# Three transfers of one batch issued by ScalarE instead of SyncE

## The chip, the cores and the metric

The kernel runs on 1 core of a Trainium2 chip. The core has TensorE (PE in the rows; its weight loads are PEld), VectorE (DVE), ScalarE (ACT), GpSimd (POOL) and SyncE (SP), which issues transfers. The metric is device time in microseconds (us) for one execution, as a median over runs. "PEclk" or the granted clock is the share of TensorE's full clock that the chip granted in a stretch: 1.00 is the 2.4 GHz level, 0.50 the 1.2 GHz level.

## The reference

The input has 8 batches of 3136 rows of 256 numbers. Each batch goes through a Fourier transform along its rows, a complex linear layer with a soft threshold, and the inverse transform. All 25088 rows then go through one expert layer:

```python
X = np.fft.rfft(x, axis=1)
Yr = Xr @ w_r - Xi @ w_i + b_r
Yi = Xr @ w_i + Xi @ w_r + b_i
Yr = np.sign(Yr) * np.maximum(np.abs(Yr) - lam, 0.0)   # Yi likewise
y = np.fft.irfft(Y, n=x.shape[1], axis=1)
...
h = x @ w_in                                           # 256 -> 1024
solu = h * softmax(h)
ln = (solu - mean) / sqrt(var + 1e-6) * g_ln
out = ln @ w_out                                       # 1024 -> 256
```

## The kernel before

A transform of length 3136 is done as 98 times 32. For every batch `b` there are four steps: `fwd1` (matmuls of 98 rows, stored to a scratch tensor in DRAM, `s1`, called `s1f` for the first two batches), `fwd2` with `mix` (the short transform and the linear layer, tile names `pb`, `Xh16`, `y`), `inv1` (the way back's short transform, whose result goes to a second scratch tensor `s2`, called `s2f` for batch 0), and `inv2` (the way back's matmuls of 98 rows, into the buffers `ring_hi`, `ring_lo`). The expert layer then takes 128 rows at a time: `moe_head` (tile `ph`, softmax in `u`), `moe_turn` (a split in two fp16 halves and a transposing transfer into `th`, `tl`) and `moe_tail` (tile `po`, output `o`). The expert layer of batch `b` runs beside the transforms of later batches. Only batch 0 has nothing to run beside: its way back must end before the first expert matmul can begin.

The scratch `s2f` of batch 0 is written by `inv1`: 128-row pieces from tile `zout`, and last the remaining 64 rows from tile `zs` (64x256 fp32, 64 KB, L821). `inv2` reads it back in groups of four columns into tile `zt` (98x1024 fp32, 392 KB, L843); there are two `zt` buffers, so the first two groups are loaded at once and the others when a buffer is free. Each group feeds 16 of PE's matmuls `pf<-iaf_s,zt`. Beside that, in the same stretch, batch 1's `fwd1` runs (loads `xt`, 392 KB; matmuls `pf<-xt,fa_s`; copies `av` on ScalarE; stores `s1f<-av`, 392 KB), and the second expert weight is prepared in quarters of 512 KB (loads `u<-in_moe_w_out`; VectorE turns its 64-bit numbers into fp32 in `th` and `tl`, GpSimd multiplies in the sign and exponent, ScalarE multiplies by `g_ln`, "th<-th,gt" and "tl<-tl,gt").

A class `Plan` records every operation and sets the order: it keeps a model of each engine and puts an operation where its model says it would start, by due times (`nc.key`). The order is then fixed for each engine, and each engine runs its own list strictly in that order; an instruction that waits for a semaphore holds back all that stands behind it on its engine. All operations are issued by `Plan.issue`, so all rows bear its line, L342. In the kernel before every transfer is issued by SyncE, on one queue.

Of the kernel before, what the change touches and what calls it, by code (L numbers as in the profile page):

```python
# [24 lines left out]
S, N1, N2 = 3136, 98, 32  # L25
H = N1 // 2
Q = (H - 1) // 2
# [424 lines left out]
def fft_mix_solu_kernel(ctx: ExitStack, tc, x, w_r, w_i, b_r, b_i, w_in, w_out, g_ln, fa, fbf, fsf, iaf, fa16, fb, fs, gb, gs, ia, out):  # L452
    nc = Plan(tc.nc)
    B, _, D = x.shape
# [18 lines left out]
    def front_psum(b):  # L473

        return banks.tile("pf" if b else "pb")
# [165 lines left out]
    s2 = {}  # L641
# [22 lines left out]
    def unit_size(u):  # L664

        return (1, 2 * N2) if u == NU - 1 else (2, P)
# [113 lines left out]
    def inv1(b, u0, u1):  # L780


        n, _ = unit_size(u0)
        half = 2 * N2
        K = half * n
        g, gi = divmod(2 * u0, QG)
        part, dtype = ((2, D), F16) if b >= PLAIN_Z else ((D,), F32)
        if n == 1:
            zo, gi = fp.tile([K, 1, *part], dtype, name="zs", bufs=1), 0
        else:  # L790
            if gi == 0:
                zouts[b] = fp.tile([P, QG, *part], dtype, name="zout")
            zo = zouts[b]
        w = u1 - u0
        pz = [front_psum(b) for _ in range(n)]
        nc.reserve(zo[:, gi : gi + n * w])
        with nc.together():
            for u in range(u0, u1):
                yh, yl = Ys.pop((b, u))
                for k, (t, j) in enumerate(((yh, 0), (yl, 0), (yh, 1))):  # L800
                    for ri in range(2):
                        for i in range(n):
                            rows = slice(i * half, (i + 1) * half)
                            gw = gs_s[:, ri, j] if n == 1 else gb_s[g][rows, u % 2, ri, j]
                            nc.tensor.matmul(
                                pz[i][:K, (u - u0) * D : (u - u0 + 1) * D], gw, t[rows, ri], start=k + ri == 0, stop=k + ri == 3
                            )
        m = n * w
        for i in range(n):
            pv = pz[i][:K, : w * D].rearrange("p (u e) -> p u e", u=w)  # L810
            if b < PLAIN_Z:
                zv = zo[:, gi : gi + m].rearrange("p (u i) e -> p u i e", i=n)[:, :, i]
                nc.scalar.activation(zv, pv, AF.Copy, scale=Z_SCALE)
                continue
            zv = zo[:, gi : gi + m].rearrange("p (u i) t e -> p u i t e", i=n)[:, :, i]
            nc.scalar.activation(zv[:, :, 0], pv, AF.Copy, scale=Z_SCALE)
            nc.vector.scalar_tensor_tensor(zv[:, :, 1], zv[:, :, 0], -LOW, pv, ALU.mult, ALU.add)
        if b >= PLAIN_Z:
            zo = zo.rearrange("p q t e -> p q (t e)")
        if n == 1:  # L820
            nc.sync.dma_start(s2[b][4 * Q :].rearrange("c (n m) -> (c n) m", n=N2), zo[:, 0])  # L821
        else:
            v = s2[b][: 4 * Q].rearrange("(q c) m -> q (c m)", c=4).rearrange("q (r m) -> r q m", r=P)
            nc.sync.dma_start(v[:, g * QG + gi : g * QG + gi + m], zo[:, gi : gi + m])
# [5 lines left out]
    G2 = 4  # L830
# [6 lines left out]
    def inv2(b, g):  # L837
        if b >= PLAIN_Z:
            zt = fp.tile([P, G2, 2, D], F16, name="zt", bufs=2)[:N1]
            nc.sync.dma_start(zt.rearrange("c n t d -> c (n t d)"), s2[b][:, g * G2 * 2 * D : (g + 1) * G2 * 2 * D])  # L840
        else:
            zt = fp.tile([P, G2, D], F32, name="zt", bufs=2)[:N1]
            nc.sync.dma_start(zt.rearrange("c n d -> c (n d)"), s2[b][:, g * G2 * D : (g + 1) * G2 * D])  # L843
        j0 = (b * N2 + g * G2) * N96 % R
        if g == 0 and b % 2 == 0:
            lasts[b // 2] = [fp.tile([P, ND, 2, N1 - N96, N2], F16, name=f"last_{part}", bufs=1) for part in ("hi", "lo")]
        for eh in range(ND):
            pa = banks.tile("pf")
            to = [
                (  # L850
                    ring[:, eh, j0 : j0 + G2 * N96].rearrange("p (i n) -> p i n", n=N96),
                    last[:, eh, b % 2, :, g * G2 : (g + 1) * G2].rearrange("p n i -> p i n"),
                )
                for ring, last in zip((ring_hi, ring_lo), lasts[b // 2])
            ]
            nc.reserve(*to[0], *to[1])
            with nc.together():
                for i in range(G2):
                    es = slice(eh * P, (eh + 1) * P)
                    if b < PLAIN_Z:  # L860
                        nc.tensor.matmul(pa[:, i * N1 : (i + 1) * N1], zt[:, i, es], iaf_s, start=True, stop=True)
                        continue
                    for k, (t, j) in enumerate(((0, 0), (0, 1), (1, 2))):
                        nc.tensor.matmul(pa[:, i * N1 : (i + 1) * N1], zt[:, i, t, es], ia_s[:, j], start=k == 0, stop=k == 2)
            pv = pa[:, : G2 * N1].rearrange("p (i n) -> p i n", n=N1)
            for hi, lo, ns in zip(*to, (slice(0, N96), slice(N96, N1))):
                nc.scalar.activation(hi, pv[:, :, ns], AF.Copy, scale=X_SCALE)
                nc.vector.scalar_tensor_tensor(lo, hi, -LOW, pv[:, :, ns], ALU.mult, ALU.add)
# [275 lines left out]
    def front_b(b, key, step):  # L1144

        lag = 4 if b == 0 else 3
        for n in range(NU + lag):
            nc.key = key + n * step
            for fn, u in ((fwd2, n), (mix, n - 1)):
                if 0 <= u < NU:  # L1150
                    fn(b, u)
            u = n - lag
            if u == NU - 1 or 0 <= u < NU and b == 0:

                inv1(b, u, u + 1)
            elif 0 < u < NU and u % 2:
                inv1(b, u - 1, u + 1)
# [20 lines left out]
    for b in range(B):  # L1178
        L = 24 + b % 2
        if b == 0:  # L1180
            front_a(1, -40, 0.5)
        if b + 2 < B:
            front_a(b + 2, first + 6, (L - 6) / 17)
        if b + 1 < B:
            front_b(b + 1, first + (6 if b == 0 else -2), (L - (8 if b == 0 else 4)) / (NU + 3))
        groups = 0
        for n in range(L):
            while groups < N2 // G2 and groups * G2 * N96 <= n * P:
                nc.key = first + n - 3
                inv2(b, groups)  # L1190
                groups += 1
            nc.key = first + n
            heads.append(moe_head((b, n if n < 24 else None)))
            nc.key = first + n + 0.5
            turned.append(moe_turn(*heads.pop(0)))
            nc.key = first + n + 1
            moe_tail(*turned.pop(0))
        first += L
# [25 lines left out]
```

## Time and profile before

| | us |
|---|---|
| median of 3 runs | 1615.39 (1613.5 to 1616.07) |
| the profiled execution's own time | 1616.65 |
| its span, first to last instruction | 1614.9 |
| PE busy in the span | 1577.4 (98%) |
| DVE busy | 1326.1 (82%) |
| ACT busy | 1238.8 (77%) |
| POOL busy | 1123.6 (70%) |
| mean DMA rate over the span | 180 GB/s |

The shares are averages over the whole span. PE is nearly always busy from 115 us on; its largest pauses lie in the first 115 us, where weights and the first batch are on their way. What a change there is worth is read from the stretch itself: which wait ends last in it.

### The profile page before, as it was taken

Reading aid. Unit: us, or ns where it says so; the run is one execution under the profiler, and the core shown is the slowest. Engines: PE = TensorE matmul, PEld = TensorE weight load, DVE = VectorE, ACT = ScalarE, POOL = GpSimd, SP = SyncE. Lnnn points to the kernel's source line nnn. Section 1 sums busy time; section 2 is a strip of 40 time slices with the busy share of each in tenths; the row PEclk is TensorE's granted clock in tenths of the full one; section 3 lists DMA queues with packets and bytes.
Section 4 is the critical chain, followed back from the end, with each engine's and each line's share of the span. In section 5 each row is a group of like instructions: output and inputs, shape, how many; then the busy total and the mean of one; then the engine's idle time right before and its main releaser. Section 6 shows DMA issues by size and latency. Waiting matters only on the chain.

```text
span 1614.9 us, 38042 instructions
## 1 busy us (share of the span) xinstructions
PE 1577.4 (98%) x13040; PEld 1126.1 (70%) x13040; DVE 1326.1 (82%) x3423; ACT 1238.8 (77%) x2576; POOL 1123.6 (70%) x1889
## 2 busy tenths in 40 slices
PE   5979999999999999999999999999999999999998
PEld 3545877678766777667776687666876677776675
DVE  4779789996799877898789978899688888877775
ACT  4667678886789867898679876798678877778886
POOL 0555776677866777667777687766976677777676
PEclk8989999999999999999999999999999999999999
DMA  8868955996579965899669984699857986677676
GB/s 236 277 228 206 210 145 133 227 240 155 127 185 232 226 151 121 185 243 217 135 130 224 279 169 118 135 246 258 166 112 165 204 172 129 122 146 154 140 129 115
DMA packets 533923, 290.25 MB, mean 180 GB/s; under 512 B 427642, under 2 KB 503964, under 8 KB 533728
## 3 DMA queue, kind: packets, MB, share of 16 engines
q1 hardware_dynamic: 533728, 287.82, 78.5%
q8 instruction: 102, 1.67, 0.4%
q14 instruction: 93, 0.76, 0.2%
HBM read 107.89 MB, written 77.07 MB: 115 GB/s over the span
## 4 chain that ended last, share of the span: by engine, by line
PE 92%; DVE 3%; ACT 2%; DMA 1%; issue 1%; POOL 0%; SPq 0%; DVEq 0%; ACTq 0%; POOLq 0%
PE po L342 31%; PE ph L342 30%; PE pf L342 27%; PE pb L342 4%; DVE u L342 1%; DVE xl L342 1%; DVE nm L342 1%; DMA zt<-s2f 0%; ACT u L342 0%; DMA s2f<-zs 0%; ACT junk L342 0%; DMA bin<-s1f 0%; DMA s1f<-tl 0%; DVE av L342 0%; DMA th<-lh 0%
## 5 line engine op out<-in xcount | busy, mean ns | idle before, releaser
L342 POOL TENSOR_TENSOR ll<-u,lh 128x1024 f16<-128x1024 f32 x196 | 424.4, 2166 | 98.5 <-ACT lh L342 95.4
L342 PE MATMUL po<-wout,th 128*128 128x256 f16 x3136 | 374.5, 273 | 4.1 <-DMA th<-lh 1.9
L342 PEld LDWEIGHTS <-th 128*128 128x128 f16 x3136 | 305.4, 98 | 64.9 <-issue 4.4
L342 ACT ACTIVATE u<-ph,m,hsb 128x512 f32<-128x512 f32 x384 | 295.9, 776 | 52.3 <-DVE m L342 51.7
L342 DVE TENSOR_REDUCE nm<-ph 128x1 f32<-128x512 f32 x392 | 264.5, 685 | 79.7 <-PE ph L342 78.6
L342 DVE SCALAR_TENSOR_TENSOR u<-ph,ch,u 128x512 f32<-128x512 f32 x392 | 281.5, 747 | 23.1 <-ACT u L342 13.7
L342 PE MATMUL ph<-win_hi,ring_hi 128*128 128x512 f16 x768 | 291.9, 380 | 0.2 <-DVE u L342 0.2
L342 PE MATMUL ph<-win_lo,ring_hi 128*128 128x512 f16 x768 | 291.5, 380 | 0.0
L342 PE MATMUL ph<-win_low,ring_lo 128*128 128x512 f16 x768 | 291.3, 379 | 0.0
L342 ACT CAST lh<-u 128x1024 f16<-128x1024 f32 x196 | 205.7, 1049 | 53.1 <-DVE u L342 52.8
L342 PEld LDWEIGHTS <-ring_hi 128*128 128x128 f16 x1536 | 146.8, 98 | 140.5 <-issue 6.5
L342 ACT ACTIVATE junk<-u,total 128x1024 bf16<-128x1024 f32 x196 | 226.1, 1154 | 7.1 <-POOL total L342 6.6
L342 PE MATMUL po<-wout,tl 128*128 128x256 f16 x1568 | 203.4, 273 | 0.8 <-DMA tl<-ll 0.8
L342 PEld LDWEIGHTS <-tl 128*128 128x128 f16 x1568 | 150.7, 98 | 35.0 <-issue 3.4
L342 POOL TENSOR_TENSOR y<-yt,yc 128x512 f32<-128x512 f32 (+1 forms) x104 | 133.1, 1281 | 59.4 <-ACT yt L342 32.7
L342 POOL TENSOR_TENSOR yl<-y,yh 128x512 f16<-128x512 f32 (+1 forms) x104 | 122.3, 1178 | 40.3 <-ACT yh L342 39.3
L342 PE MATMUL pf<-w_hi,Xh 128*128 128x256 f16 (+1 forms) x546 | 149.1, 273 | 0.0
L342 PE MATMUL pf<-w_hi,Xl 128*128 128x256 f16 (+1 forms) x546 | 148.9, 273 | 0.0
L342 PE MATMUL pf<-w_lo,Xh 128*128 128x256 f16 (+1 forms) x546 | 148.8, 273 | 0.0
L342 ACT ACTIVATE o<-po,r 128x256 f32<-128x256 f32 x196 | 93.2, 475 | 59.6 <-PE po L342 30.7
L342 PEld LDWEIGHTS <-ring_lo 128*128 128x128 f16 x768 | 75.1, 98 | 91.1 <-DVE last_lo L342 0.3
L342 PEld LDWEIGHTS <-Xh 128*128 128x128 f16 (+1 forms) x1196 | 113.9, 99 | 24.8 <-issue 1.9
(196 smaller groups left out, 2922.5 us busy)
## 6 DMA issues: line engine op xcount, KB each, us to landing
xt<-in_x_dram SPq DMA_DIRECT2D x108, 392.0 KB
zt<-s SPq DMA_DIRECT2D x56, 392.0 KB
s<-zout SPq DMA_DIRECT2D x42, 512.0 KB
s<-av SPq DMA_DIRECT2D x48, 392.0 KB
bin<-s SPq DMA_DIRECT2D x36, 512.0 KB
out_dram<-o SPq DMA_DIRECT2D x128, 96.0 KB
out_dram<-o SPq DMA_DIRECT2D x136, 64.0 KB
bin<-s1f SPq DMA_DIRECT2D x12, 512.0 KB
```

The costliest lines, as they stand in the source:

```text
L342: getattr(engine, name)(*args, **kw)
```

## The change

The store of tile `zs` of batch 0 and the loads of `zt` for the first two groups of batch 0 are issued by ScalarE, on ScalarE's own queue, instead of SyncE. The loads of batch 0's six other groups, and all of the other batches, stay with SyncE. `Plan` places the three transfers in ScalarE's list like any of its operations.

```diff
         if n == 1:
-            nc.sync.dma_start(s2[b][4 * Q :].rearrange("c (n m) -> (c n) m", n=N2), zo[:, 0])
+            (nc.sync if b else nc.scalar).dma_start(s2[b][4 * Q :].rearrange("c (n m) -> (c n) m", n=N2), zo[:, 0])
...
             zt = fp.tile([P, G2, D], F32, name="zt", bufs=2)[:N1]
-            nc.sync.dma_start(zt.rearrange("c n d -> c (n d)"), s2[b][:, g * G2 * D : (g + 1) * G2 * D])
+            (nc.scalar if g < 2 else nc.sync).dma_start(zt.rearrange("c n d -> c (n d)"), s2[b][:, g * G2 * D : (g + 1) * G2 * D])
```

On ScalarE, where the way forth of batch 0 has ended, the list reads as follows (`+` is what the change adds; `zs` is the tile of 64 rows, `av` batch 1's copies, `th` and `tl` quarters of the second expert weight, which GpSimd writes just before):

```order
 L342 ACTIVATE zs<-pb 64x256
 L342 ACTIVATE win_low<-win_hi 128x1024
+L342 DMA s2f<-zs 64x256
 L342 COPY av<-pf 98x512 x4
 L342 ACTIVATE th<-th,gt 128x256 x2
+L342 DMA zt<-s2f 98x1024 x2
 L342 ACTIVATE tl<-tl,gt 128x256 x2
 L342 COPY av<-pf 98x512 x2
```

The store stands two places behind the activation that fills `zs`; the two loads stand behind four copies and behind the two activations on `th`.

On SyncE, at the same place of the program (`u` is a quarter of the second expert weight in its raw form), the list loses the three:

```order
 L342 DMA s2f<-zout 128x2x256
-L342 DMA u<-in_moe_w_out_dram 128x2x512
-L342 DMA s2f<-zs 64x256
-L342 DMA u<-in_moe_w_out_dram 128x2x512
+L342 DMA u<-in_moe_w_out_dram 128x2x512 x2
 L342 DMA s1f<-av 98x1024
 L342 DMA xt<-in_x_dram 98x1024
 L342 DMA s1f<-av 98x1024
-L342 DMA zt<-s2f 98x1024 x2
 L342 DMA xt<-in_x_dram 98x1024
 L342 DMA s1f<-av 98x1024
```

What stood behind them moves up; its own order is unchanged. On PE, VectorE and GpSimd the order of the instructions is the same in both kernels.

## Rows read from the trace of the kernel before

**Rows 1.** The page's first part: busy us, share of the span, instructions.

```profile
PE 1577.4 (98%) x13040; PEld 1126.1 (70%) x13040; DVE 1326.1 (82%) x3423; ACT 1238.8 (77%) x2576; POOL 1123.6 (70%) x1889
```

**Rows 2.** The chain of work that ended last, 98 to 150 us: start, us, what.

```profile
102.59 5.21 DMA s2f<-zs
...
107.87 6.95 DMA zt<-s2f
...
122.07 2.38 PE ph L342 x6
```

**Rows 3.** Timeline of PE: start, us, operation, count, [idle before <-what ended it].

```profile
100.61 5.39 PE L342 MATMUL pf<-xt,fa_s 98*98 98x512 f32 x12
114.95 7.12 PE L342 MATMUL pf<-iaf_s,zt 98*128 98x98 f32 x32 [8.95 <-DMA zt<-s2f]
```

**Rows 4.** Timeline of ScalarE.

```profile
103.39 2.19 ACT L342 COPY av<-pf 98x512 f32<-98x512 f32 x4
111.03 0.91 ACT L342 ACTIVATE th<-th,gt 128x256 f32<-128x256 f32 x2 [5.46 <-POOL th L342]
112.25 0.91 ACT L342 ACTIVATE tl<-tl,gt 128x256 f32<-128x256 f32 x2 [0.32 <-POOL tl L342]
...
116.65 0.91 ACT L342 ACTIVATE th<-th,gt 128x256 f32<-128x256 f32 x2 [2.54 <-POOL th L342]
```

**Rows 5.** Timeline of GpSimd.

```profile
105.93 5.07 POOL L342 TENSOR_TENSOR th<-th,ll 128x512 f32<-128x512 f32 x1 [5.97 <-DVE th L342]
...
115.34 1.28 POOL L342 TENSOR_TENSOR th<-th,ll 128x512 f32<-128x512 f32 x1 [3.13 <-DVE th L342]
```

**Rows 6.** L342 from 112.2 to 112.5 us: ScalarE's sequencer; ns min/median/max, first and last start.

```profile
L342 ACTq EVENT_SEMAPHORE  x2: 17/28/38, 112.3 to 112.4; - x2
```

**Rows 7.** Timeline of SyncE: start of an issue, us, transfer.

```profile
103.16 0.53 SPq L342 DMA_DIRECT2D u<-in_moe_w_out_dram  x1
104.48 0.34 SPq L342 DMA_DIRECT2D s1f<-av  x1
104.91 0.34 SPq L342 DMA_DIRECT2D xt<-in_x_dram  x1
105.60 0.82 SPq L342 DMA_DIRECT2D s1f<-av  x1
107.87 1.32 SPq L342 DMA_DIRECT2D zt<-s2f  x2
109.29 0.40 SPq L342 DMA_DIRECT2D xt<-in_x_dram  x1
```

**Rows 8.** Transfers from 107 to 115 us: packets, bytes, mean rate.

```profile
DMA packets 742, 2.46 MB, mean 307 GB/s; under 512 B 86, under 2 KB 94, under 8 KB 742
```

**Rows 9.** The same chain, 28 to 40 us.

```profile
30.78 3.47 DMA s1f<-tl
...
34.31 3.81 DMA bin<-s1f
```

**Rows 10.** Timeline of VectorE.

```profile
109.45 0.42 DVE L342 TENSOR_SCALAR lh<-u 128x512 uint32<-128x512 uint32 x1
...
116.31 0.68 DVE L342 TENSOR_REDUCE mx<-tl 128x1 f32<-128x512 f32 x1
```

**Rows 11.** Stretches: us, busy us (instructions) by engine, PEclk, DMA share, GB/s.

```profile
38.10:42.20 4.10, 4.03 (x19) 4.04 (x20) 0.75 (x1) 0.90 (x2) 0.00 (x0) 0.50 0.96 323
42.20:46.00 3.80, 3.80 (x22) 2.13 (x22) 2.17 (x4) 1.16 (x2) 0.00 (x0) 1.00 0.72 235
...
114.90:122.00 7.10, 7.05 (x33) 7.06 (x34) 7.10 (x16) 3.39 (x10) 2.55 (x2) 0.50 0.72 234
122.00:124.10 2.10, 2.10 (x7) 0.73 (x6) 1.27 (x4) 1.35 (x4) 0.00 (x0) 0.50 0.53 148
124.10:131.00 6.90, 6.90 (x26) 2.84 (x24) 5.83 (x25) 3.23 (x7) 0.00 (x0) 1.00 0.54 159
131.00:146.00 15.00, 14.14 (x71) 7.81 (x71) 14.65 (x47) 12.69 (x26) 11.09 (x18) 1.00 0.81 202
```

## The prediction

> **What bounds the kernel now.** I began with the page's busy shares: PE is busy for 1577.4 of 1614.9 us [rows 1], so over most of the span only work taken off PE would help, and the change takes none off. What it can move is a pause of PE. The chain of work that ended last shows one that goes through both kinds of transfer that are moved: the store of `zs`, issued at 102.59, takes 5.21 us to land; the first load of `zt` is issued at 107.87 and lands 6.95 us later, at 114.82 [rows 2]. PE's timeline shows the same from its side: the last `pf<-xt` group starts at 100.61 and lasts 5.39 us, to 106.0, and the next one, `pf<-iaf_s,zt`, starts at 114.95 after 8.95 us idle, ended by that load [rows 3]. So the moment at which the first `zt` lands is the quantity to forecast. From there on the chain is PE again (7.12 us of `pf`, then `ph`), and in 131 to 146 us VectorE is busy for 14.65 of 15.00 us and PE for 14.14 [rows 11]: there is next to no slack in which a later or earlier start could vanish, so I pass a shift of that moment on to the end one to one.
>
> **The store of `zs` on ScalarE.** The store can be issued from about 102.6, when `zs` is filled, or at the latest when ScalarE's next activation is over and the copies start, at 103.39 [rows 4]. No row shows a transfer issued by ScalarE. Its landing is bounded by the 5.21 us of the busy SyncE queue [rows 2] above and by 3.47 us, the store that the chain waited for at 30.78 with little else queued [rows 9], below: it lands between 106.1 and 108.6. I take the early end, since the data volume is only 64 KB. Either end turns out not to matter, because of what follows. Issuing takes ScalarE's queue a fraction of a microsecond (SyncE needs 0.3 to 0.8 us for one [rows 7]); even several microseconds would be hidden, since ScalarE waits for 5.46 us before 111.03 [rows 4], and the copies it would delay (103.39 to 105.6) are needed by PE's banks only at 114.95.
>
> **The two loads of `zt` on ScalarE.** Here the order decides. On ScalarE they stand behind the two activations `th<-th,gt`. Those start at 111.03, since they wait for GpSimd [rows 4]: its `th<-th,ll` starts at 105.93 and takes 5.07 us, where the same operation at 115.34 takes 1.28 [rows 5]. So the loads can't be issued at 107.87 any more. ScalarE's sequencer runs ahead of its datapath: when the first `tl` activation started at 112.25, it stood at the waits of the copies behind both of them at 112.3, and each wait took 17 to 38 ns [rows 4, 6]. By that the loads' waits are reached just after 111.03; with four or five such waits I put the first issue at 111.35 (111.94 if the queue should hold until both activations are over). Their other waits are met by then: the store has landed by 108.6, and the second load's wait is for the third `u` load, which VectorE reads at 109.45 without idling [rows 10].
>
> How long from issue to landing? Below: 3.81 us, the load `bin<-s1f` of 512 KB for which the chain waited with little ahead of it [rows 9]. Above: 6.95 us, the same load on the busy queue [rows 2]. The difference, 3.14 us, is what stood ahead of it; at the mean 307 GB/s of that stretch [rows 8] this is 0.96 MB, a little over half of the 1.73 MB (one `u` of 0.524 MB, three of 0.401 MB) issued from 103.16 to 105.60 [rows 7]. In the changed kernel SyncE's next `xt` load (0.401 MB), issued at 109.29 behind `zt` [rows 7], moves up to about 106.4, so ahead of ScalarE's loads stand 1.36 MB at 107.87. By 111.35, 3.48 us later, 1.07 MB of it are gone and 0.29 MB left: 0.96 us if they all go first, nothing if the two queues take turns from the start. The first `zt` lands between 111.35 + 3.81 = 115.16 and 116.1; with the late issue at 111.94 the rest is 0.11 MB, and it is again 116.1. I take the middle, 115.6, since row and rest are equally near. That is **0.8 us later** than 114.82. The second `zt` follows with 1.3 us (0.401 MB at that rate), and PE needs it only half of 7.12 us after the first.
>
> The Trainium skill speaks on this twice. "DMA: Bandwidth & Descriptors", section "Issuing engines are not separate DMA queues", says that transfers from any issuer run on the same 16 DMA engines and that a second issuer saves only issue time: by it the load has the whole rest ahead of it, and the sum would be at its upper end, 116.1. The same page's "Queues, rings and completion order" says that each DMA engine serves its queues in turn: by it the lower end. No run before this has two such queues.
>
> **What stands behind.** The pair of issues occupies ScalarE's queue for about 1.32 us, SyncE's time for it [rows 7]: until 112.7 instead of 112.25 for `tl<-tl,gt`, and as much for the copies after it. That is covered: the reader `mx<-tl` starts at 116.31 [rows 10], and ScalarE itself waits 2.54 us before 116.65 [rows 4]. If that cover were gone it would cost 0.4 us. On SyncE the `xt` load and the stores behind it move up; no instruction of the chain waits for them, so I cost it at nothing.
>
> **TensorE's clock.** In the pause the granted clock fell to 0.50 (the 1.2 GHz level) and was still there for the 7.10 us of `pf<-iaf_s,zt`; it was 0.50 to 124.1 and 1.00 after [rows 11], 9.15 us after PE began again. After the earlier pause it came back at 42.2, 4.1 us after the restart [rows 11]. The rows don't say which of the two the changed kernel will meet. If it returned after 4.1 us, 5.05 us of half pace would be saved, worth at most 2.5 us; as much is the most I allow on the other side. The forecast takes 9.15 us again.
>
> **Sum.** 0 (store) + 0.8 (first `zt`) + 0 (ScalarE's queue) + 0 (SyncE) = +0.8 us. Against the profiled execution's own 1616.65 us (span 1614.9 and 1.75 around it) that is 1617.45. That execution lies 1.26 us above the median of the three runs, 1615.39, so the predicted median is **1616.2**.
>
> **Rivals.** (a) The clock returns late: 2.5 us on top, 1618.7. For it: PE begins later, and its `pf<-iaf_s,zt` stretch did not bring the clock back before. Against: it returned soon after the `ph` matmuls had begun. (b) The clock returns early: 1613.7. (c) Slower, at one place: ScalarE's loads get no turn of their own, and first pay for a queue as full as SyncE's was, 6.95 us. Issued at 111.35, `zt` lands at 118.3, 3.5 us later: 1618.9. It decides from a landing after 118.05. Against it: only 0.29 MB are left by then. (d) Faster: GpSimd's `th` takes 1.28 us, as its other instance did [rows 5]. Then ScalarE's `th` starts at 107.2, the loads are issued at 107.55, and with turns of their own land at 111.36, 3.46 us earlier: 1611.9. Against it: nothing in the change touches GpSimd or VectorE, whose order is the same, and the long instance ends only when VectorE's run of operations on `u` does (109.45 + 0.42 us [rows 10]). (e) The change doesn't do what it says: the loads wait on ScalarE for something other than the store. That is the forecast itself, GpSimd's operation taking the place of the store as the last wait.
>
> **How the numbers follow.** Forecast 0.65 (within 0.2%); (a) 0.13, half of it over 0.2%; (b) 0.08, within; (c) 0.07, slower; (d) 0.05, faster; 0.02 for a shift of either sign in the ramp after 131 us. 0.2% is 3.2 us, about what a measurement of this kernel can tell from no change. Faster 0.06, within 0.79, slower 0.15. The landing's bounds, 115.16 and 116.1, give 1615.7 and 1616.7; with the clock's 2.5 us on either side the range is 1613.2 to 1619.2, which takes in (a), (b) and (c) and leaves out (d).
>
> **What would show it.** In the changed profile: the two loads in ScalarE's queue right behind its `th`, near 111.3 and 111.8 (right) or near 107 (wrong, rival d); the first `pf<-iaf_s,zt` at 115.3 to 116.2, its idle ended by `zt`, with GpSimd's `th` and ScalarE's `th` ahead of the load in the chain, and the store gone from it; the store landed before 108.6; `tl<-tl,gt` at most 0.5 us later; the clock at 1.00 about 9 us after PE's restart. The forecast is wrong if `zt` lands before 114.5 or after 116.5, or if the ramp in 131 to 146 us swallows the shift.

## The result, and the profile after

The changed kernel takes **1618.6 us** (median of 20 runs, 1614.26 to 1621.3). The kernel before takes 1614.28 us beside it (20 runs, 1612.25 to 1616.6). The ratio, worked out over all runs, is 1.0022, with a 95% interval of 1.0015 to 1.0028: the change costs 2.4 to 4.5 us. Single runs of one kernel spread by several us, so kernels are compared here over many runs. The time lies within the predicted range but 2.4 us above the forecast. A loss of 0.22% is just past the 0.2% from which the prediction counted a kernel as slower, a case that it gave 0.15; the interval takes in both sides of that line. The profiled execution took 1618.42 us (span 1616.6), against 1616.65 (span 1614.9).

PE's timeline answers to [rows 3]; columns are start, us, operation, count, [idle before <-what ended it]:

```profile
99.73 5.39 PE L342 MATMUL pf<-xt,fa_s 98*98 98x512 f32 x12
115.34 7.12 PE L342 MATMUL pf<-iaf_s,zt 98*128 98x98 f32 x32 [10.22 <-ACT av L342]
```

All starts lie a little earlier here: the `pf<-xt` group starts at 99.73 instead of 100.61. So what is to be compared is the pause itself: **10.22 us instead of 8.95, 1.27 us longer**. The row names ScalarE's copy `av` as its end, but only because that copy happens to end at the same time. In a second profile of the same kernel (`e6_after_again`, below) the same matmuls start before that copy does, and the row names `zt`.

ScalarE answers to [rows 4]; "ACTq" rows are transfers that it issues:

```profile
101.71 0.51 ACTq L342 DMA_DIRECT2D s2f<-zs  x1
105.80 0.91 ACT L342 ACTIVATE th<-th,gt 128x256 f32<-128x256 f32 x2 [1.05 <-POOL th L342]
107.18 1.62 ACTq L342 DMA_DIRECT2D zt<-s2f  x2
110.11 0.91 ACT L342 ACTIVATE tl<-tl,gt 128x256 f32<-128x256 f32 x2 [3.40 <-POOL tl L342]
```

GpSimd's `th` (which answers to [rows 5]), and then the operation of VectorE that comes next to it in time:

```profile
104.49 1.27 POOL L342 TENSOR_TENSOR th<-th,ll 128x512 f32<-128x512 f32 x1 [5.42 <-DVE th L342]
```

```profile
104.85 1.22 DVE L342 TENSOR_REDUCE peaks<-xt 98x1 f32<-98x1024 f32 x1 [0.44 <-DMA xt<-in_x_dram]
```

Two things differ from the forecast. GpSimd's `th` took 1.27 us and not 5.07, so ScalarE's `th` was done at 106.7, and the loads were issued at 107.18 and not at 111.35. And yet the first `zt` came at about the moment of the forecast: PE starts at 115.34, 8.16 us after the issue. The loads left 2.06 us into the pause (107.18 against 105.12, the end of `pf<-xt`). In the kernel before they left 1.87 us into it and took 6.95 us [rows 2].

What the transfers did in these 8 us is seen in the queues' rows of two stretches, 107 to 111 and 111 to 115 us (q1 is SyncE's queue, q10 ScalarE's; packets, MB, share of the 16 DMA engines' time). First 107 to 111:

```profile
q1 hardware_dynamic: 402, 1.36, 86.9%
q10 hardware_dynamic: 8, 0.03, 2.0%
```

Then 111 to 115:

```profile
q10 hardware_dynamic: 193, 0.71, 59.4%
q1 hardware_dynamic: 142, 0.48, 36.5%
```

For nearly four us after the issue SyncE's transfers take the DMA engines almost alone (402 packets against 8). Part of this is the load's own start: in e5 below, where SyncE has little left, ScalarE's queue moved 5 packets in the first 1.1 us after the issue. SyncE's transfers include the `xt` load that used to stand behind `zt`:

```profile
104.77 0.35 SPq L342 DMA_DIRECT2D s1f<-av  x1
105.22 1.70 SPq L342 DMA_DIRECT2D xt<-in_x_dram  x1
```

In [rows 7] the order is `s1f`, `zt`, `xt`. Now `xt` is issued 1.96 us before `zt`.

Last the stretches, which answer to [rows 11] (us, busy us and instructions of PE, PEld, DVE, ACT, POOL; PEclk; DMA share; GB/s):

```profile
109.50:115.30 5.80, 0.00 (x0) 0.00 (x0) 5.80 (x13) 3.23 (x8) 1.84 (x2) 0.50 0.93 307
115.30:126.50 11.20, 11.16 (x40) 8.56 (x41) 6.88 (x15) 3.62 (x12) 1.27 (x1) 0.50 0.49 161
126.60:131.00 4.40, 4.40 (x17) 1.81 (x15) 3.15 (x11) 1.95 (x4) 0.00 (x0) 1.00 0.49 142
131.00:146.00 15.00, 15.00 (x74) 8.09 (x74) 14.54 (x51) 12.59 (x26) 9.70 (x17) 1.00 0.77 207
```

After the restart PE runs 11.2 us at the 1.2 GHz level (115.3 to 126.5), where before it ran 9.2 us (to 124.1 [rows 11]). Two us more at half pace are 1.0 us of work lost. Pause and clock together make 1.27 + 1.0 = 2.3 us. The first `po` of the expert layer shows the same sum. In the chain it starts at 147.26:

```profile
147.26 2.78 PE po L342 x24
```

In the chain of the kernel before the same step reads:

```profile
145.87 2.78 PE po L342 x24
```

That is 42.14 us after the end of `pf<-xt` now, and 39.87 us after it before: 2.27 us more. Nothing was given back in the ramp from 131 to 146 us, where VectorE is again busy for 14.54 of 15.00 us.

### The profile page after: what moved, and what is told of

It reads as the page before. It is cut to its first block, busy times and chain, and to the rows that moved or that the text cites. A ratio compares the mean times of both kernels' runs of the same rounds, so it can differ in the third digit from the quotient of the medians.

```text
span 1616.6 us, 38037 instructions
## 1 busy us (share of the span) xinstructions
PE 1581.1 (98%) x13040; PEld 1128.0 (70%) x13040; DVE 1324.2 (82%) x3423; ACT 1240.0 (77%) x2576; POOL 1122.6 (69%) x1889
## 3 DMA queue, kind: packets, MB, share of 16 engines
HBM read 107.89 MB, written 77.07 MB: 114 GB/s over the span
## 4 chain that ended last, share of the span: by engine, by line
PE 91%; DVE 4%; ACT 1%; DMA 1%; issue 1%; POOL 1%; SPq 0%; DVEq 0%; ACTq 0%; POOLq 0%
PE po L342 31%; PE ph L342 29%; PE pf L342 27%; PE pb L342 4%; DVE u L342 1%; DVE nm L342 1%; DMA tl<-ll 1%; DVE av L342 0%; DVE xl L342 0%; ACT u L342 0%; POOL ll L342 0%; ACT junk L342 0%; DMA bin<-s1f 0%; DVE ring_lo L342 0%; DMA s1f<-tl 0%
## 5 line engine op out<-in xcount | busy, mean ns | idle before, releaser
L342 POOL TENSOR_TENSOR ll<-u,lh 128x1024 f16<-128x1024 f32 x196 | 425.7, 2172 | 97.7 <-ACT lh L342 96.2
L342 PE MATMUL po<-wout,th 128*128 128x256 f16 x3136 | 376.1, 273 | 3.9 <-DMA th<-lh 1.6
L342 PEld LDWEIGHTS <-th 128*128 128x128 f16 x3136 | 306.1, 98 | 65.5 <-issue 4.4
L342 ACT ACTIVATE u<-ph,m,hsb 128x512 f32<-128x512 f32 x384 | 296.1, 777 | 50.5 <-DVE m L342 49.9
L342 DVE TENSOR_REDUCE nm<-ph 128x1 f32<-128x512 f32 x392 | 264.8, 686 | 80.5 <-PE ph L342 79.4
L342 DVE SCALAR_TENSOR_TENSOR u<-ph,ch,u 128x512 f32<-128x512 f32 x392 | 281.5, 748 | 22.8 <-ACT u L342 13.3
L342 PE MATMUL ph<-win_hi,ring_hi 128*128 128x512 f16 x768 | 291.9, 380 | 0.2 <-DVE u L342 0.2
L342 PE MATMUL ph<-win_low,ring_lo 128*128 128x512 f16 x768 | 291.5, 380 | 0.0
L342 PE MATMUL ph<-win_lo,ring_hi 128*128 128x512 f16 x768 | 291.5, 380 | 0.0
L342 ACT CAST lh<-u 128x1024 f16<-128x1024 f32 x196 | 205.7, 1050 | 52.9 <-DVE u L342 52.6
L342 PEld LDWEIGHTS <-ring_hi 128*128 128x128 f16 x1536 | 146.8, 98 | 140.4 <-issue 6.5
L342 ACT ACTIVATE junk<-u,total 128x1024 bf16<-128x1024 f32 x196 | 226.2, 1154 | 7.2 <-POOL total L342 6.8
L342 PE MATMUL po<-wout,tl 128*128 128x256 f16 x1568 | 203.4, 273 | 1.1 <-DMA tl<-ll 0.9
L342 PEld LDWEIGHTS <-tl 128*128 128x128 f16 x1568 | 150.7, 98 | 35.6 <-issue 3.6
L342 POOL TENSOR_TENSOR y<-yt,yc 128x512 f32<-128x512 f32 (+1 forms) x104 | 133.2, 1283 | 58.5 <-ACT yt L342 32.1
L342 POOL TENSOR_TENSOR yl<-y,yh 128x512 f16<-128x512 f32 (+1 forms) x104 | 122.3, 1178 | 40.1 <-ACT yh L342 39.4
L342 PE MATMUL pf<-w_hi,Xh 128*128 128x256 f16 (+1 forms) x546 | 149.1, 273 | 0.0
L342 PE MATMUL pf<-w_hi,Xl 128*128 128x256 f16 (+1 forms) x546 | 148.8, 273 | 0.0
L342 PE MATMUL pf<-w_lo,Xh 128*128 128x256 f16 (+1 forms) x546 | 148.8, 273 | 0.0
L342 ACT ACTIVATE o<-po,r 128x256 f32<-128x256 f32 x196 | 93.3, 476 | 61.0 <-PE po L342 32.2
L342 PEld LDWEIGHTS <-ring_lo 128*128 128x128 f16 x768 | 75.1, 98 | 91.1 <-issue 0.5
L342 PEld LDWEIGHTS <-Xh 128*128 128x128 f16 (+1 forms) x1196 | 114.0, 99 | 24.7 <-issue 1.9
```

Of the source, the lines that this page charges most:

```text
L342: getattr(engine, name)(*args, **kw)
```

## The experiments

Two parts of the change can be at fault (the store, the loads), and three causes: that the loads stand behind ScalarE's `th` and so behind GpSimd; that SyncE's bytes get to the DMA engines first; and TensorE's clock, which falls in the pause and can turn a small delay into a larger one. Each experiment is timed against the kernel before in runs of the same chip; the figure behind "Measured" is the ratio to it, with its 95% interval.

### The parts by themselves: e1 and e2

```diff
-            nc.sync.dma_start(s2[b][4 * Q :].rearrange("c (n m) -> (c n) m", n=N2), zo[:, 0])
+            (nc.sync if b else nc.scalar).dma_start(s2[b][4 * Q :].rearrange("c (n m) -> (c n) m", n=N2), zo[:, 0])
```

> Only the store of zs goes to ScalarE; SyncE keeps the two loads of zt, at their old place. Theory Q (the queue itself is no faster: in the changed kernel the store was issued at 101.71 and ScalarE could issue the load that waits for it only at 107.18, 5.4 us later, as 5.2 us before): within 0.5 us of the kernel before, first zt matmul about 9 us after the last xt matmul. Rival S (the store is what costs, since ScalarE's queue starts slowly): 2 us slower or more. If the store gained from its own queue: up to 2 us faster, since the load is issued when it has landed.

Measured: 1.0003 (0.9993 to 1.0013). The chain of waits, then PE's row:

```profile
102.20 6.68 DMA s2f<-zs
108.96 5.09 DMA zt<-s2f
```

```profile
114.19 7.12 PE L342 MATMUL pf<-iaf_s,zt 98*128 98x98 f32 x32 [8.56 <-DMA zt<-s2f]
```

The store alone costs nothing that can be measured. It isn't quick on ScalarE's queue either: 64 KB took 6.68 us to land, against 5.21 on SyncE's [rows 2]. The load behind it gave the time back (5.09 us instead of 6.95).

```diff
-            nc.sync.dma_start(zt.rearrange("c n d -> c (n d)"), s2[b][:, g * G2 * D : (g + 1) * G2 * D])
+            (nc.scalar if g < 2 else nc.sync).dma_start(zt.rearrange("c n d -> c (n d)"), s2[b][:, g * G2 * D : (g + 1) * G2 * D])
```

> Only the two loads of zt go to ScalarE, behind its activations on th; the store stays on SyncE. Theory L (the loads' place and queue carry the whole loss): as the changed kernel, 3 to 4.5 us slower than before, PE's pause ended by zt 10 to 12 us long. Rival S (the store carries it): within 1 us of before.

Measured: 1.0012 (1.0003 to 1.002). Chain, PE's row and two stretches:

```profile
105.92 8.08 DMA zt<-s2f
```

```profile
114.14 7.12 PE L342 MATMUL pf<-iaf_s,zt 98*128 98x98 f32 x32 [10.86 <-DMA zt<-s2f]
```

```profile
114.10:124.90 10.80, 10.76 (x40) 8.55 (x41) 7.04 (x16) 3.77 (x12) 1.27 (x1) 0.50 0.53 180
125.00:130.00 5.00, 5.00 (x19) 2.08 (x18) 3.45 (x14) 2.34 (x4) 0.00 (x0) 1.00 0.50 150
```

The profile of the loads alone shows what that of the whole change shows: a load of 8.08 us, a pause of 10.86 us, and 10.8 us at half pace behind it. By time they cost 1.9 us (0.5 to 3.2), less than the 3 to 4.5 expected; this interval and that of the change overlap.

### Loads ahead of `th`: e3

In the changed kernel, the two loads are put ahead of the first activation `th<-th,gt` in ScalarE's list. For that `Plan` gets a list of moves, each of which puts one operation ahead of another once the order is made; the other operations keep theirs:

```diff
+    moved = lambda self, order: [order.insert(order.index(at), order.pop(order.index(op))) for op, at in self.moves] and order
...
-        order = self.order()
+        order = self.moved(self.order())
...
-            (nc.scalar if g < 2 else nc.sync).dma_start(zt.rearrange("c n d -> c (n d)"), s2[b][:, g * G2 * D : (g + 1) * G2 * D])
+            op = (nc.scalar if g < 2 else nc.sync).dma_start(zt.rearrange("c n d -> c (n d)"), s2[b][:, g * G2 * D : (g + 1) * G2 * D]); g < 2 and nc.moves.append((op, nc.marks["th"]))
...
-                nc.scalar.activation(row, row, AF.Copy, scale=gt[:, i : i + 1])
+                nc.marks.setdefault("th", nc.scalar.activation(row, row, AF.Copy, scale=gt[:, i : i + 1]))
```

> As the changed kernel, but the two loads stand in ScalarE's list ahead of the activations on th, so they wait for the store alone and never for GpSimd. Theory G (the loss comes from the executions in which GpSimd's operation on th takes 5 us instead of 1.3, so that the loads are issued near 111 us): the loss falls to 1 to 2 us and the spread of the times with it. Theory Q (queue and bytes ahead): no better than the changed kernel, 3 to 4.5 us slower than before.

Measured: 1.0019 (1.0008 to 1.0031). GpSimd's row, the chain's step and PE's row:

```profile
104.80 5.09 POOL L342 TENSOR_TENSOR th<-th,ll 128x512 f32<-128x512 f32 x1 [6.38 <-DVE th L342]
```

```profile
107.89 6.76 DMA zt<-s2f
```

```profile
114.78 7.12 PE L342 MATMUL pf<-iaf_s,zt 98*128 98x98 f32 x32 [10.31 <-DMA zt<-s2f]
```

Here GpSimd is held for 5.09 us and the loads don't wait for it (they are issued at 107.89, while it runs), but nothing is won: the pause is 10.31 us. The loads left 3.42 us into it, later than in the changed kernel, 6.84 us after the issue of the store at 101.05; the chain names an `xt` load that lands at that moment, so whether the store or that load held them isn't shown. That GpSimd holds up the loads, the core of my second step, is not what makes the changed kernel slower: in its own two profiles (the one above and e6), and in e2, w2 and w5, GpSimd's `th` takes 1.26 to 1.28 us.

### The bytes ahead, without ScalarE: e4

In the kernel before, with everything on SyncE, only the `xt` load of batch 1's last piece (`c` = 7) is put ahead of the first `zt` load, by such a move:

```diff
...
-            nc.sync.dma_start(zt.rearrange("c n d -> c (n d)"), s2[b][:, g * G2 * D : (g + 1) * G2 * D])
+            op = nc.sync.dma_start(zt.rearrange("c n d -> c (n d)"), s2[b][:, g * G2 * D : (g + 1) * G2 * D]); g or nc.moves.append((nc.marks[1, 7], op))
```

> The kernel before, all transfers on SyncE, with one change: batch 1's last xt load (0.401 MB) is issued ahead of the two zt loads instead of behind them, the order in which the changed kernel's bytes were queued. Theory Q (bytes ahead): zt lands 1.3 us later, PE's pause 10.2 instead of 8.95 us, and the kernel is 1.3 us slower, 2 to 3 us if the clock comes back later for it. Rival P (what costs is a slow start of ScalarE's queue, not the bytes): under 1.5 us, well below the 3.5 us of the changed kernel.

Measured: 1.001 (1.0 to 1.0019).

```profile
108.72 7.38 DMA zt<-s2f
```

```profile
116.23 7.12 PE L342 MATMUL pf<-iaf_s,zt 98*128 98x98 f32 x32 [9.51 <-DMA zt<-s2f]
```

The 0.401 MB ahead lengthen the load from 6.95 to 7.38 us and the pause by 0.56 us, to 9.51 where 10.2 was expected. That is somewhat under half of the 1.27 us of the changed kernel. That the rest comes with ScalarE's queue isn't shown: w3 below, the same order with PE kept at work, has a longer load on SyncE's queue than any on ScalarE's. The clock returned 8.4 us after the restart, so nothing was added by it.

### The bytes behind: e5

In the changed kernel, that `xt` load is put ahead of batch 2's first load, and so behind SyncE's next store `s1f`, which waits for ScalarE:

```diff
...
-        nc.sync.dma_start(t, x[b].rearrange("s d -> (s d)").rearrange("(p c n) -> c p n", p=P, c=NPK)[c])
+        nc.marks[b, c] = nc.sync.dma_start(t, x[b].rearrange("s d -> (s d)").rearrange("(p c n) -> c p n", p=P, c=NPK)[c]); (b, c) == (2, 0) and nc.moves.append((nc.marks[1, 7], nc.marks[2, 0]))
```

> The changed kernel with one thing undone: SyncE's last xt load of batch 1 is issued behind the next s1f store, so it no longer stands ahead of the zt loads. No fillers. Theory Q+C (the bytes ahead lengthen the pause, the longer pause keeps the clock at half pace longer): PE's pause 9 to 9.5 us instead of 10.2, 0 to 1 us slower than before. If ScalarE's queue or GpSimd's operation carries the loss: as the changed kernel, 3 us or more slower.

Measured: 1.0012 (0.9999 to 1.0026), which doesn't tell it from the kernel before, nor from the changed kernel. Its profiled run was a long one (span 1620.7 us), and I found no cause for the part of that beyond this stretch. The stretch itself is plain. ScalarE's rows, the chain, and PE's row:

```profile
110.74 0.51 ACT L342 ACTIVATE th<-th,gt 128x256 f32<-128x256 f32 x1 [5.04 <-POOL th L342]
110.90 0.61 ACTq L342 DMA_DIRECT2D zt<-s2f  x1
```

```profile
110.90 4.80 DMA zt<-s2f
```

```profile
115.83 7.12 PE L342 MATMUL pf<-iaf_s,zt 98*128 98x98 f32 x32 [9.55 <-DMA zt<-s2f]
```

This is the prediction's second step but for the `xt` load, which no longer stands ahead: GpSimd held, the load issued just behind `th` and landing after 4.80 us. I had bounded that by 3.81 and 4.75 with the `xt` load ahead; without it, the prediction's sum would have left nothing ahead and taken 3.81. From 111 to 115 us most transfers are ScalarE's:

```profile
q10 hardware_dynamic: 200, 0.76, 62.7%
q1 hardware_dynamic: 57, 0.18, 11.5%
```

So a load on ScalarE's queue takes 4.8 us where SyncE has little left and 8.1 where SyncE has bytes standing. The pause, 9.55 us, is 0.6 us longer than before. That this is close to the 0.8 that I had is luck, since the load took longer than its bound with less ahead of it.

### The changed kernel again: e6

> The changed kernel once more, on the chip of this call, for a common yardstick and a second profile: 3 to 4.3 us slower than before, PE's pause 10 us or longer, the second stretch at half pace 17 us long instead of 13.7.

Measured: 1.0017 (1.0008 to 1.0025). Chain, PE and ScalarE:

```profile
99.69 5.08 DMA s2f<-zs
...
104.87 8.13 DMA zt<-s2f
```

```profile
113.14 7.12 PE L342 MATMUL pf<-iaf_s,zt 98*128 98x98 f32 x32 [10.03 <-DMA zt<-s2f]
```

```profile
113.35 1.05 ACT L342 COPY av<-pf 98x512 f32<-98x512 f32 x2
```

PE starts at 113.14, ahead of the copies at 113.35, and the row names `zt`: the pause ends with that load. The chain goes through the store, whose landing releases the load, and through 8.13 us of load. The whole stretch at half pace, from the fall of the clock in the pause to its return, is 17.1 us long, as expected.

### PE kept at work through the pause: w1 to w6

To take the clock out of the comparison, PE gets matmuls that nobody needs: 58 in an earlier pause of batch 0 (in `fwd2`), and 38 (w1 to w4) or 48 (w5, w6) ahead of the first `pf<-iaf_s,zt`, in the bank that the real matmuls then overwrite (the profile counts each of these matmuls twice). The order of everything else stays the same.

```diff
+            warm = 38 if (b, g, eh) == (0, 0, 0) else 0
...
+                for _ in range(warm):
+                    nc.tensor.matmul(pa[:, :P], ones, ones, start=True, stop=True)
```

First the kernel before (w1) and the changed one (w2) with 38; w3 is e4 with them and w4 is e5 with them.

> The kernel before with filler matmuls (results unused, 128x128 fp32) on PE in its two pauses: 58 ahead of batch 0's first short transform, 38 ahead of the first way-back matmul, so that PE works while it waits. The granted clock should stay 1.00 through both. Theory C (half pace after the pauses is part of every execution and varies): 3 to 6 us faster than before (7.1 us of pf and 2.1 us of ph at half pace, and 4.1 us after the first pause, each worth up to half), and a narrower spread. If the ramp behind is bound by VectorE anyway: under 1 us.

> The changed kernel with the same fillers. Theory C (most of the change's loss is the clock that comes back later after a longer pause): 1 to 1.5 us behind the kernel before with fillers, the difference of the two pauses (10.2 against 8.95 us) alone. Theory Q (bytes ahead and ScalarE's queue carry the whole loss): 3 to 4 us behind it.

> The kernel before with the xt load ahead of the zt loads, all on SyncE, with the same fillers. Bytes ahead alone: 0.5 to 1.3 us behind the kernel before with fillers. If it is as far behind as the changed kernel with fillers, ScalarE's queue adds nothing of its own.

> The changed kernel with fillers, and SyncE's xt load put behind the next s1f store, so that it is issued after the zt loads and the bytes ahead of them are those of the kernel before. If the bytes ahead make the longer pause: level with the kernel before with fillers, within 0.5 us. If ScalarE's queue has a slow start of its own (issue at 107.18, zt landed by 115.2): still 0.7 us or more behind it.

Measured: w1 0.9982 (0.9972 to 0.9992), w2 0.9995 (0.9982 to 1.0009), w3 0.9985 (0.9975 to 0.9995), w4 0.9972 (0.9961 to 0.9983). PE's rows of w2:

```profile
102.78 8.65 PE L342 MATMUL pf<-ones 128*128 128x128 f32 x76
112.85 3.81 PE L342 MATMUL pf<-iaf_s,zt 98*128 98x98 f32 x32 [1.42 <-DMA zt<-s2f]
```

The real matmuls now take 3.81 us instead of 7.12, since the clock stays at 1.00; in these two rows w1 differs only in the idle time behind the fillers (1.09 us). But w2 keeps the clock in some runs only. Its three runs with a mean granted clock of 1.000 took 1609.7 to 1611.14 us, and the two lowest, at 0.995, took 1618.01 and 1619.27. So in this kernel time and clock go together, and the size fits: 0.005 of 1615 us is 8.1 us. Whether a longer pause came first in the slower runs isn't shown, as they have no profile. The medians of w2 and w1 lie 1.7 us apart, but their intervals overlap, so theories C and Q aren't told apart by time. w1 is 2.9 us (1.3 to 4.5) faster than the kernel before, at the low end of what theory C had for it.

The four profiles answer what e4 left open. From the end of `pf<-xt` to the first `pf<-iaf_s,zt` it takes 9.59 us in w1, 9.91 in w2, 10.27 in w3 and 9.26 in w4. So with fillers the `xt` load ahead costs 0.68 us where the loads are on SyncE (w3 against w1) and 0.65 where they are on ScalarE (w2 against w4). Without fillers it was 0.56 (e4 against before) and 0.48 to 0.67 (e6 and the change against e5). ScalarE's queue in place of SyncE's goes with 0.5 to 0.7 us more without fillers, but with 0.3 to 0.4 us less with them. Each kernel has one profile, the change two. The cost of the `xt` load ahead is much the same in all these pairs, about half of the 1.27 us; a cost of ScalarE's queue isn't shown. In w3, SyncE's rows and PE's:

```profile
103.66 0.92 SPq L342 DMA_DIRECT2D xt<-in_x_dram  x1
104.67 1.73 SPq L342 DMA_DIRECT2D zt<-s2f  x2
```

```profile
113.37 3.81 PE L342 MATMUL pf<-iaf_s,zt 98*128 98x98 f32 x32 [1.78 <-DMA zt<-s2f]
```

So on SyncE's own queue the load took about 8.6 us. Its time goes with the bytes that all queues move between its issue and its landing: 1.17 MB in 4.8 us (e5), 2.16 in 6.9 (before), 2.58 in 8.0 (the change) and 2.62 in 8.6 (w3).

With 48, the fillers outlast the pause:

> The changed kernel with fillers as before, but 48 instead of 38 in the second pause (about 10.4 us of work at full pace), so that PE is busy for the whole pause also where it is longer. Theory C (the clock is what spreads and slows the executions): time at half pace falls to the 2 us of the kernel before with fillers, the spread shrinks from 9.6 to under 5 us, and the time is within 1 us of w6. If the pause itself carries the loss: 1.5 us or more behind w6.

> The kernel before with 58 and 48 fillers, the yardstick for w5. Its pause is about 9.6 us, so the longer filler may hold the way back up by up to 0.8 us: 0 to 1 us slower than with 38 fillers, 2 to 4 us faster than the kernel before.

```profile
104.64 10.88 PE L342 MATMUL pf<-ones 128*128 128x128 f32 x96
115.36 3.71 PE L342 MATMUL pf<-iaf_s,zt 98*128 98x98 f32 x32
```

These are PE's rows of w5, the changed kernel; PE doesn't idle, the granted clock is 1.00 from 100 to 130 us, and w6 has the same two lengths and the same clock. Measured: **w5 0.9984 (0.9975 to 0.9993), w6 0.9983 (0.9974 to 0.9992)**. Where the pause is filled in both and the clock stays, the change costs nothing that can be measured: the medians, 1613.36 and 1612.64 us, lie 0.7 us apart. Each interval is 2.9 us wide, so a rest of one to two us isn't ruled out. As far as these runs can tell, the loss lies in PE's pause and in the half pace behind it, not in ScalarE's or SyncE's lists later on. The spread is not all the clock's: w5's runs still lie 7.1 us apart, where under 5 was expected.

All kernels with fillers but w2 are faster than the kernel before. The best is w4, 1611.81 us. Its interval overlaps that of w1, which has nothing of the change, so I put the gain down to the fillers.

## Why the prediction went as it did

Working the two terms out for every profile without fillers (pause, plus half of the us at 0.50 after the restart, as the stretches show them) gives what each should cost against the kernel before, beside what the runs gave (the ratio's excess times 1615 us):

| kernel | pause | us at 0.50 after it | pause + half | against before | measured |
|---|---|---|---|---|---|
| before | 8.95 | 9.2 | 13.55 | | |
| the change | 10.22 | 11.2 | 15.82 | +2.3 | +3.6 (2.4 to 4.5) |
| e6, the change again | 10.03 | 11.3 | 15.68 | +2.1 | +2.7 (1.3 to 4.0) |
| e1, store only | 8.56 | 9.5 | 13.31 | -0.2 | +0.5 (-1.1 to 2.1) |
| e2, loads only | 10.86 | 10.8 | 16.26 | +2.7 | +1.9 (0.5 to 3.2) |
| e3, loads first | 10.31 | 8.8 | 14.71 | +1.2 | +3.1 (1.3 to 5.0) |
| e4, `xt` ahead | 9.51 | 8.4 | 13.71 | +0.2 | +1.6 (0 to 3.1) |
| e5, `xt` behind | 9.55 | 11.6 | 15.35 | +1.8 | +1.9 (-0.2 to 4.2) |

One profile stands for a dozen runs here. Most rows agree within that; the change (first profile) and e3 fall just short of their intervals, and about 2 us of e3 stay unexplained.

- **The range**: in part luck. The three runs under the forecast lie 1.1 us above the median of the 20. Taken by itself the change cost 3.6 us by the ratio and 4.3 by the medians, against a forecast of 0.8 and an upper end of the range that is 3.8 us above its own start. The moment of the first `zt`, 115.2, lies within the 114.5 to 116.5 that were to show the forecast right, but by two errors that cancel (the loads, below).
- **What bounds the kernel**: right. The moment of the first `zt` set the time, and a shift of it was passed on (2.27 us at the first `po`); w5 and w6 show nothing else of the change that counts.
- **The store, 0**: right in its price (e1), wrong in its size and in why it wouldn't matter. I took the early end of 3.47 to 5.21 us; it took at most 5.5 us in the changed kernel (from its issue to that of the load that waits for it), 5.08 in e6 and 6.68 in e1. And it stayed in the chain of e6, since the load waited for it and not for GpSimd.
- **The loads, +0.8**: this is a term that was mis-sized; it measured +1.27 and +1.08 in the two profiles. Both halves of its working failed, in opposite directions. The issue came 4 us earlier than at 111.35, because GpSimd's `th` was short: the condition of rival (d). The landing took 8.1 us instead of 3.81 to 4.75: the mechanism of rival (c), since at 107.18 the bytes of SyncE that I expected to be gone by 111.35 were still there. The prediction's own rows would have given that price. Its 1.36 MB ahead take 4.4 us at its 307 GB/s [rows 8], and 4.4 + 3.81 is 8.2. What I didn't do was to work rival (d) through with the queue as full as it is at that earlier moment. I let it land after 3.81 us and so made it the one fast case. Issued 4 us earlier, the load landed no earlier, since the DMA engines had no time for it yet.
- **ScalarE's queue and SyncE, 0 each**: ScalarE's is right as put (the issues took 1.62 us, hidden in a wait of 3.40 us). Of SyncE the prediction said that the `xt` moving up costs nothing because no instruction of the chain waits for it. It stands in the way of one that does: e4 puts 0.56 us of pause on that alone, and the other pairs above 0.48 to 0.68.
- **The clock, "9.15 us again"**: this step failed. It took 11.2 us, 1.0 us of work, and as much in e6. Rival (a), to which I gave 0.13, is the case that came, with a price of 1.0 us instead of 2.5 on top of a larger landing term. The kernels with SyncE's loads (before, e1, e4) had 8.4 to 9.5 us at half pace behind the pause. Those with ScalarE's had 10.8 to 11.6, but for e3 with 8.8. The whole stretch at half pace, counted from the fall of the clock in the pause, sorts them without exception: 13.6 to 13.7 us in the first three, 17.0 to 17.1 in the other five. In e3 it began earlier in the pause, so less of it lay behind the restart. What decides between the two lengths isn't shown; the length of the pause alone doesn't, since e4 paused for 9.51 us and e5 for 9.55. I had two returns in [rows 11], after 4.1 and 9.15 us, and these were a reason to give another one more than 0.13.

The prediction set two sections of the Trainium skill's "DMA: Bandwidth & Descriptors" against each other. "Issuing engines are not separate DMA queues" says that transfers of any issuer run on the same 16 DMA engines and interleave there; that the load has the whole rest ahead of it is more than it states. "Queues, rings and completion order" says that each DMA engine serves its queues in turn. The changed kernel's trace fits neither reading from start to end: 402 packets against 8 in the four us after the issue aren't turns, and 142 against 193 in the next four aren't one queue wholly behind the other. Behind a nearly empty SyncE (e5) both give the same.

**What stays open.** The difference between the 2.3 us of the two terms and the 3.6 us measured lies at the edge of the interval. What makes up the half of the longer pause that the `xt` load doesn't explain isn't shown, nor what sets the length of the stretch at half pace. Why VectorE had to wait for its `xt` (0.44 us) in the changed kernel and not in the one before, at the same operation, isn't settled. Nor is e5, whose interval takes in both answers.

## What to carry to other kernels

Before a transfer is moved to another engine's queue, count the bytes that every queue has standing at the new moment of issue, those included that move up into the gap: the 16 DMA engines are shared, and here a load took 4.8 us behind little and about 8 us or more behind a full queue, issued by ScalarE (the change, e2, e6) or by SyncE (w3). A long pause of PE costs its length and the half pace behind it, so price both, and look at filling it: matmuls for nobody in two pauses won 0.17% (0.08 to 0.26) here (w6; which of the two pauses gave it wasn't tried), where no move of a transfer won anything by itself. And when a rival changes one number of a sum, work the whole sum again with it.

## What the runs showed that I had not expected

GpSimd's `th<-th,ll` of this stretch takes either 1.26 to 1.28 us (the change, e6, e2, w2, w5) or 5.05 to 5.09 (the other nine profiles), and which of the two goes with who starts first. If VectorE's next operation (`peaks<-xt`) starts before it, by 0.12 to 0.18 us, GpSimd is held to the end of VectorE's run of operations. If GpSimd starts first, even by 0.02 us, it is done at once. This held in all 14 profiles. The closest pair is w1 and w2: GpSimd starts at 102.32 and at 102.31, VectorE at 102.15 and at 102.33. GpSimd and VectorE of w1:

```profile
102.32 5.05 POOL L342 TENSOR_TENSOR th<-th,ll 128x512 f32<-128x512 f32 x1 [5.43 <-DVE th L342]
```

```profile
102.15 1.22 DVE L342 TENSOR_REDUCE peaks<-xt 98x1 f32<-98x1024 f32 x1
```

And of w2:

```profile
102.31 1.28 POOL L342 TENSOR_TENSOR th<-th,ll 128x512 f32<-128x512 f32 x1 [5.41 <-DVE th L342]
```

```profile
102.33 1.22 DVE L342 TENSOR_REDUCE peaks<-xt 98x1 f32<-98x1024 f32 x1
```

The prediction read "nothing in the change touches GpSimd or VectorE, whose order is the same" as a reason against rival (d). The order was the same; between w1 and w2, less than 0.2 us made the difference.

A head start of `peaks<-xt` alone doesn't hold GpSimd, though. The same operation on the next quarter takes 1.28 us at 115.34 in the kernel before [rows 5], although VectorE's `peaks<-xt` starts 0.16 us ahead of it there too:

```profile
115.18 1.21 DVE L342 TENSOR_REDUCE peaks<-xt 98x1 f32<-98x1024 f32 x1
```

So it is in all 14 profiles. Behind `peaks<-xt` comes another reduction there (`mx<-tl`), and not the run of operations on `u`. Which operation holds GpSimd isn't settled.

The Trainium skill's "SBUF — State Buffer", section "SBUF: two separate sides", describes a port pair that these two engines share and that whichever starts first holds for its whole instruction; of VectorE's operations it names those in a 2-port mode or with two inputs. The traces agree that the two engines hold each other up (5.05 us in w1 against 1.28 in w2). They don't agree that the first to start decides: in w1 GpSimd had started before seven of the eight operations of VectorE that it waited through, and the first, a reduction with one input, didn't hold it on the next quarter.
